# Router steps over more iterations, gate parts ahead of the subtractions, divisions ahead of weight pieces, other banks at the transition

## The chip, the cores and the metric

The kernel runs on one core of a Trainium2 chip. The metric is the device time of one execution in microseconds. The profile is one execution, taken by the hardware profiler. Its engines are TensorE (PE, and PEld for its weight loads), VectorE (DVE), ScalarE (ACT), GpSimd (POOL) and SyncE (SP, which issues most DMAs). Each engine works through its own queue in order.

## The reference

Attention over 8 batches of 576 tokens with 8 heads of 64: the first four heads see the last 32 positions, the last four see every 32nd position. The result, 4608 tokens of 512, goes through a mixture of experts: a token whose skip score is positive is given to the expert with the largest logit, passes its two layers, and the result times the gate is added to the token.

```python
scores = scale * q @ k.T, masked per head (local or strided)
attn = exp(scores - max);  attn = attn / (attn.sum(-1) + 1e-09)
x = (attn @ v) as [4608, 512]
do_compute = x @ w_skip > 0
e_idx = argmax(xc @ w_gate);  gate_w = softmax(xc @ w_gate)[e_idx]
h = relu(xc[mask] @ w1[e]);  y[mask] = gate_w * (h @ w2[e])      # 8 experts
out[do_compute] = xc + y
```

## The kernel before

**Attention.** The work of a batch is cut into four units `pr` 0 to 3 (`UNITS`): 0 and 1 are the local heads (5 and 4 blocks), 2 and 3 the strided heads (6 and 5 blocks). The loop at L860 runs over 32 iterations (b, pr). One iteration issues, in an order that each engine keeps:

- `qk` of the unit two iterations ahead: score matmuls into a pair of banks with the tag S (there is one such pair), the mask addition on VectorE that reads it (L211 local, L214 strided), the maximum (L220), and two subtractions on GpSimd (L222);
- `tex` of this unit: transposes (L242) and the exponential on ScalarE (L250);
- `score` of the batch before, in one iteration of each batch (L337, copies at L342 and L344);
- `xpose` of the unit two back: transposes of the finished x (L319) and copies (L321);
- `pv` of the unit one back: products with v (L276), then on VectorE the reciprocal of the sums (L285, L286) and the two divisions (L292), one for each bank of the pair PV.

**Router.** Every two batches make a group of nine tiles of 128 tokens. `route1` (end of batches 2, 4 and 6; for the last group at the transition) transposes the router scores (L361), finds each token's expert and leaves the sum of exponentials `zs`, made on GpSimd (L399 to L401). `route2` in (3,0), (5,0) and (7,0) (table `RANKS`) counts ranks with matmuls, takes the reciprocal of `zs` (L418), works out positions on VectorE (L420 to L432) and the gate in three bf16 parts on GpSimd (L435 to L440, `rpo` at L442). `onehots` (table `ONES`: (3,1), (5,1), (7,0)) makes two products on VectorE, `roh` (L453) and `rx` (L456); `rx` reads `rpo`. `tabled` (table `TABS`: (3,3), (5,3), (7,1)) multiplies them on TensorE (L464) and adds the result to `acc` (L468, L470). `pick` in (5,0) chooses an expert after batch 3 (L518 to L534); SyncE loads its number in (5,2) and uses it for the weight loads of this expert "e" (L602; three buffers `raw`). Its pieces are cast on ScalarE (`wcast`, L613) and the remainder made on VectorE (`wrest`, L619); `CASTS`, `RESTS` and `FETCH` say in which iterations. In (7,1) `chosen` takes the token indices of expert "e" from `acc` (`ei`, L492), and three indirect DMAs on GpSimd gather its tokens (L644).

**Transition (L920 to L934).** The last unit's products go to the pair S. Its divisions come after the remainder of weight piece 4; then piece 5 is cast and its remainder made, the gathered tokens are turned (`xturn`, L666 to L669) around the turn of the last x, and the last scores are made (L337).

**FFN.** A second PSUM pool (L937) has four banks S, three T and one R; its places follow the order in which the tags are first asked for. The first FFN matmuls of expert "e" (`ffn1a`, L711, L715; outputs at L684, L685) come first, then `route1`'s second half for the last group, `route2`, `onehots`, `tabled`. From about 187 us on the kernel runs through the experts' two layers (L672 to L674) to its end.

## Time and profile before

| what | us |
|---|---|
| median of 3 runs (lowest, highest) | 438.48 (437.18, 439.31) |
| the profiled execution | 436.99 |
| its span, first to last instruction | 435.2 |
| TensorE busy in it | 401.0 |
| VectorE busy in it | 272.2 |
| ScalarE busy in it | 202.5 |
| GpSimd busy in it | 125.6 |

The profiled execution is 1.8 us longer than its span; sums over the trace are made against it, and the median lies 1.5 us above it. Attention takes the first 160 us, the transition and the last group's router the next 27, the experts the rest.

### The profile page before, as it was taken

To read this page: it belongs to the slowest core of one execution; us is meant where nothing else is said; L and a number is where in the kernel's file an instruction comes from. 1 tells how busy PE (TensorE), PEld (TensorE's weight loads), DVE (VectorE), ACT (ScalarE), POOL (GpSimd) and SP (SyncE) were. 2 spreads that over 40 slices of the span, in tenths; PEclk is the share of its full clock that TensorE was granted. 3 is DMA by queue.
4 is the path that set the end of the run, shared out by engine and by line. 5 is a ranking of instruction groups with operands and counts; after the bars stand their busy time and mean duration, and the time that the engine had idled before them with its cause. 6 is when DMAs were issued, how large, how long until landed. Compare 5 with 4: busy or idle time off the path is not lost.

```text
span 435.2 us, 12084 instructions
## 1 busy us (share of the span) xinstructions
PE 401.0 (92%) x4975; PEld 364.2 (84%) x4976; DVE 272.2 (63%) x548; ACT 202.5 (47%) x384; POOL 125.6 (29%) x161
## 2 busy tenths in 40 slices
PE   5989799897879687999999999999999999999994
PEld 3878777787667464899898899999999999999984
DVE  3676669878968854872694563474564754755610
ACT  1557546584577255404533353544444445545300
POOL 2442334435323540250133144032042141201201
PEclk9799989999999878999999999999999999999999
DMA  8999978998896246034376567366466566636101
GB/s 278 397 386 313 316 233 274 304 291 296 258 372 196 58 137 172 2 104 131 104 234 187 164 222 193 132 202 205 149 201 191 161 215 194 205 130 196 42 20 44
DMA packets 49707, 86.05 MB, mean 198 GB/s; under 512 B 7050, under 2 KB 26890, under 8 KB 49648
## 3 DMA queue, kind: packets, MB, share of 16 engines
q1 hardware_dynamic: 43248, 74.87, 53.3%
q0 software_dynamic: 6400, 10.36, 8.3%
q8 instruction: 40, 0.66, 0.6%
q14 instruction: 19, 0.16, 0.1%
HBM read 70.88 MB, written 14.90 MB: 197 GB/s over the span
## 4 chain that ended last, share of the span: by engine, by line
PE 76%; DVE 14%; issue 3%; DMA 2%; ACT 2%; POOL 1%; SPq 1%; POOLq 0%; DVEq 0%
PE S L672 16%; PE S L674 16%; PE S L673 16%; PE PV L276 5%; PE T L242 5%; PE S L204 5%; PE T L319 3%; DVE x L292 2%; PE T L666 2%; PE PV L764 2%; PE T L337 2%; DMA kt<-in_kp_dram 1%; DVE mx L220 1%; DVE rx L456 1%; DVE frame L214 1%
## 5 line engine op out<-in xcount | busy, mean ns | idle before, releaser
L672 PE MATMUL S<-xh,w1h 128*128 128x342 f32 (+6 forms) x248 | 78.1, 315 | 0.0
L674 PE MATMUL S<-xh,w1l 128*128 128x342 f32 (+6 forms) x248 | 76.4, 308 | 0.0
L673 PE MATMUL S<-xl,w1h 128*128 128x342 f32 (+6 forms) x248 | 76.4, 308 | 0.0
L672 PE MATMUL S<-hh,w2h 128*128 128x288 f32 (+5 forms) x192 | 59.3, 309 | 0.6 <-DVE hl L685 0.6
L674 PE MATMUL S<-hh,w2l 128*128 128x288 f32 (+5 forms) x192 | 58.0, 302 | 0.0
L673 PE MATMUL S<-hl,w2h 128*128 128x288 f32 (+5 forms) x192 | 57.8, 301 | 0.0
L684 ACT ACTIVATE hh<-S 128x342 fp32r<-128x342 f32 (+6 forms) x64 | 27.8, 436 | 63.5 <-PE S L674 58.4
L752 POOL DMA_INDIRECT out_dram<-ot,n1i x18 | 19.3, 1070 | 116.9 <-DVE ot L750 115.4
L619 DVE TENSOR_TENSOR w1l<-raw,w1h 128x1024 fp32r<-128x1024 f32 x32 | 39.0, 1223 | 18.5 <-ACT w1h L613 17.7
L672 PEld LDWEIGHTS S<-xh,w1h 128*128 128x128 f32 x248 | 46.8, 189 | 0.3 <-issue 0.2
L673 PEld LDWEIGHTS S<-xl,w1h 128*128 128x128 f32 x248 | 46.7, 188 | 0.1
L674 PEld LDWEIGHTS S<-xh,w1l 128*128 128x128 f32 x248 | 46.7, 188 | 0.0
L619 DVE TENSOR_TENSOR w2l<-raw,w2h 128x1024 fp32r<-128x1024 f32 x32 | 39.1, 1223 | 10.0 <-ACT w2h L613 8.9
L204 PE MATMUL S<-kt,qt 64*64 64x54 f32 (+1 forms) x1280 | 34.7, 248 | 10.3 <-DMA kt<-in_kp_dram 3.5
L222 POOL TENSOR_TENSOR sm<-sm,mx 128x480 f32<-128x480 f32 (+1 forms) x32 | 28.4, 908 | 52.3 <-DVE mx L220 21.1
L204 PEld LDWEIGHTS S<-kt,qt 64*64 64x64 f32 x1280 | 29.0, 146 | 14.5 <-DVE sm L211 5.2
L685 DVE SCALAR_TENSOR_TENSOR hl<-S,hh 128x342 fp32r<-128x342 f32 (+6 forms) x64 | 30.5, 482 | 14.9 <-ACT hh L684 14.8
L250 ACT ACTIVATE ptl<-T 96x512 f32<-96x512 f32 (+1 forms) x40 | 19.9, 546 | 42.1 <-PE T L242 42.1
L672 PEld LDWEIGHTS S<-hh,w2h 128*128 128x128 f32 x192 | 36.2, 188 | 0.8 <-DVE hl L685 0.8
L673 PEld LDWEIGHTS S<-hl,w2h 128*128 128x128 f32 x192 | 36.3, 189 | 0.0
L674 PEld LDWEIGHTS S<-hh,w2l 128*128 128x128 f32 x192 | 36.1, 188 | 0.0
L730 ACT COPY yT<-S 128x288 f32<-128x288 f32 (+5 forms) x24 | 9.9, 412 | 55.9 <-PE S L674 47.0
(215 smaller groups left out, 813.3 us busy)
## 6 DMA issues: line engine op xcount, KB each, us to landing
raw<-in_w_dram SPq DMA_DIRECT2D x64, 512.0 KB
vt<-in_vp_dram SPq DMA_DIRECT2D x24, 390.0 KB
qt<-in_qp_dram SPq DMA_DIRECT2D x16, 304.0 KB
kt<-in_kp_dram SPq DMA_DIRECT2D x16, 297.0 KB
out_dram<-x SPq DMA_DIRECT2D x16, 288.0 KB
kt<-in_kp_dram SPq DMA_DIRECT2D x14, 304.0 KB
qt<-in_qp_dram SPq DMA_DIRECT2D x14, 288.0 KB
out_dram<-x SPq DMA_DIRECT2D x32, 99.0 KB
```

Of the source, the lines that this page charges most:

```text
L204: T.matmul(s[HP * (i ^ j):HP * (i ^ j) + HP, j, (blk - b0) * win:(blk - b0 + 1) * win], lhsT=qt[p, j, blk * nq:blk * nq + HP], rhs=kt[p, j ...
L222: G.tensor_tensor(e[:, j], e[:, j], mx[:, j].unsqueeze(2).broadcast_to([128, b1 - b0, win]), op=ALU.subtract)
L242: T.transpose(t[:w, x * 128:(x + 1) * 128], a, ident)
L250: A.activation(pt[:w, (g + x) * 128:(g + y) * 128], t[:w, x * 128:y * 128], AF.Exp, scale=0.125)
L276: T.matmul(p[HP * i:HP * i + HP, bank, slot * 65:slot * 65 + 65], lhsT=pt[a:z, m, j, i ^ j, :], rhs=vt[a:z, b0 // 2 + m if kind else (b0 + ...
L619: V.tensor_tensor(lo, raw_.pop((key, j)), hi.bitcast(F32), op=ALU.subtract)
L672: T.matmul(p, lhsT=a[0], rhs=b[0], start=start, stop=False)
L673: T.matmul(p, lhsT=a[0], rhs=b[1], start=False, stop=False)
L674: T.matmul(p, lhsT=a[1], rhs=b[0], start=False, stop=stop)
L684: A.activation(s["hh"][:, f, :C], p[:, :C], AF.Relu)
L685: V.scalar_tensor_tensor(s["hl"][:, f, :C], p[:, :C], 0.0, s["hh"][:, f, :C].bitcast(F32), op0=ALU.max, op1=ALU.subtract)
L752: i = G.indirect_dma_start(out=out, in_=ot[:P], in_offset=None, bounds_check=NTOK - 1, oob_is_err=False, out_offset=bass.IndirectOffsetOnA ...
```

## The change

- `scaled` makes one division in place of two where both banks hold the same number of slots: units 0, 1 and 2 of every batch; unit 3 keeps two.
- `gated` is cut out of `route2`: the reciprocal, the gate's parts and `rpo`. In (3,0), (5,0) and (7,0) it is issued within `qk`, after the mask addition and ahead of the maximum and the subtractions; for the last group ahead of the FFN's first outputs.
- `operands` (`rx`) is cut out of `onehots` and gets a table of its own; `onehots` and `tabled` move to later iterations, `pick` from (5,0) to (5,1), `chosen` and the gathers from (7,1) to (7,2).
- At the transition the last divisions come directly after their products, ahead of the remainder of piece 4; the cast of piece 4 moves there from (7,3); the cast and remainder of piece 5 move behind all turns of the gathered tokens.
- A tile of tag T and one of tag R are asked for ahead of the FFN's sums, so that T and R take the first four banks of the pool and S the last four.

```diff
--- before.py
+++ after.py
@@ -43,13 +43,14 @@
 ESTR = 5120
 ROUND = 1.5 * 2.0 ** 23
 RANKS = {(3, 0): 0, (5, 0): 1, (7, 0): 2}
-ONES = {(3, 1): 0, (5, 1): 1, (7, 0): 2}
-TABS = {(3, 3): 0, (5, 3): 1, (7, 1): 2}
+ONES = {(3, 1): 0, (5, 2): 1, (7, 1): 2}
+OPERANDS = {(3, 2): 0, (5, 3): 1, (7, 1): 2}
+TABS = {(4, 0): 0, (6, 0): 1, (7, 2): 2}
 COUNTED = {1: 3, 2: 5}
 PB = 3
 CB = 5
 EG = 2
-CASTS = [(6, 0), (6, 1), (7, 0), (7, 2), (7, 3)]
+CASTS = [(6, 0), (6, 1), (7, 0), (7, 2)]
 RESTS = [(6, 1), (6, 2), (7, 2), (7, 3)]
 FETCH = [(6, 0), (6, 1), (6, 3), (7, 0), (7, 3)]
 CE = (96, 3)
@@ -264,13 +265,11 @@
         if kind == 0:
             jobs = [(0, LW, m, j, j, m) for m in range(n) for j in range(2)]
             slots = (n, n)
-            outs = [x[:, :, 64 * j:64 * j + 64] for j in range(2)]
         else:
 
             jobs = [(HP * o, HP * o + SQ, m, j, o, 2 * m + j) for m in range((n + 1) // 2)
                     for o in range(2) for j in range(2) if 2 * m + o < n]
             slots = (n + 1) // 2 * 2, n // 2 * 2
-            outs = [x[:, o::2, :].rearrange("p m (j d) -> p m j d", j=2) for o in range(2)]
         for a, z, m, j, bank, slot in jobs:
             for i in range(2):
                 T.matmul(p[HP * i:HP * i + HP, bank, slot * 65:slot * 65 + 65], lhsT=pt[a:z, m, j, i ^ j, :],
@@ -284,12 +283,20 @@
             u = slots[z.start]
             V.tensor_scalar_add(rc[:, z, 0:u], pw[:, z, 0:u, 64], 1e-9)
             V.reciprocal(rc[:, z, 0:u], rc[:, z, 0:u])
-        for o in range(2):
-            u = slots[o]
-            num, den = pw[:, o, 0:u, 0:64], rc[:, o, 0:u].unsqueeze(2).broadcast_to([128, u, 64])
+        def scaled(to, z, u):
+            num = pw[:, z, 0:u, 0:64]
+            den = rc[:, z, 0:u].unsqueeze(3).broadcast_to([128, z.stop - z.start, u, 64])
             if kind:
-                num, den = (y.rearrange("p (m j) d -> p m j d", j=2) for y in (num, den))
-            V.tensor_tensor(outs[o], num, den, op=ALU.mult)
+                num, den = (y.rearrange("p o (m j) d -> p o m j d", j=2) for y in (num, den))
+            V.tensor_tensor(to, num, den, op=ALU.mult)
+
+        if kind == 0:
+            scaled(x.rearrange("p n (j d) -> p j n d", j=2), slice(0, 2), n)
+        elif n % 2 == 0:
+            scaled(x.rearrange("p (m o) (j d) -> p o m j d", o=2, j=2), slice(0, 2), w)
+        else:
+            for o in range(2):
+                scaled(x[:, o::2, :].rearrange("p m (j d) -> p m j d", j=2).unsqueeze(1), slice(o, o + 1), slots[o])
 
     def store(b, kind):
         ob = out[b * S:(b + 1) * S, kind * 256:kind * 256 + 256]
@@ -401,8 +408,25 @@
         G.tensor_scalar(zs, zs, 1e-9, None, op0=ALU.add)
         rt_[g] = [nt, sp, ohb, h, zs, tally if last else None]
 
+    def gated(g):
+        nt, sp, ohb, h, zs, tally = rt_[g]
+        at = slice(GA[g], GA[g] + nt)
+        gate = gates[:, at]
+        V.reciprocal(gate, zs)
+        p3 = pc[:, at]
+        G.tensor_copy(p3[:, :, 2], gate)
+        r = sp("rr", [128, nt])
+        G.tensor_tensor(r, gate, p3[:, :, 2], op=ALU.subtract)
+        G.tensor_copy(p3[:, :, 3], r)
+        G.tensor_tensor(r, r, p3[:, :, 3], op=ALU.subtract)
+        G.tensor_copy(p3[:, :, 4], r)
+        po = sp("rpo", [128, nt, 5, NE], BF16)
+        G.tensor_tensor(po, p3.unsqueeze(3).broadcast_to([128, nt, 5, NE]),
+                        ohb.unsqueeze(2).broadcast_to([128, nt, 5, NE]), op=ALU.mult)
+        rt_[g][4] = po
+
     def route2(g, tag="T", of=None):
-        nt, sp, ohb, h, zs, tally = rt_[g]
+        nt, sp, ohb, h, po, tally = rt_[g]
         rk = ps(tag)
         rkv = rk[:, 0:nt * NE].rearrange("p (t e) -> p t e", e=NE)
         T.matmul(rkv, lhsT=tri, rhs=ohb, start=True, stop=False)
@@ -414,8 +438,6 @@
             summed(of, rk[:, nt * NE:(nt + 1) * NE])
         yield
         at = slice(GA[g], GA[g] + nt)
-        gate = gates[:, at]
-        V.reciprocal(gate, zs)
         dd = sp("rdd", [128, nt, NE])
         V.tensor_tensor(dd, rkv, ohb, op=ALU.mult)
         ds = dsall[:, at]
@@ -431,16 +453,6 @@
         V.scalar_tensor_tensor(m3, nv, -3.0, ds, op0=ALU.mult, op1=ALU.add)
         V.tensor_tensor(n3, m3.unsqueeze(2).broadcast_to([128, nt, 3]),
                         con["n3"].unsqueeze(1).broadcast_to([128, nt, 3]), op=ALU.is_equal)
-        p3 = pc[:, at]
-        G.tensor_copy(p3[:, :, 2], gate)
-        r = sp("rr", [128, nt])
-        G.tensor_tensor(r, gate, p3[:, :, 2], op=ALU.subtract)
-        G.tensor_copy(p3[:, :, 3], r)
-        G.tensor_tensor(r, r, p3[:, :, 3], op=ALU.subtract)
-        G.tensor_copy(p3[:, :, 4], r)
-        po = sp("rpo", [128, nt, 5, NE], BF16)
-        G.tensor_tensor(po, p3.unsqueeze(3).broadcast_to([128, nt, 5, NE]),
-                        ohb.unsqueeze(2).broadcast_to([128, nt, 5, NE]), op=ALU.mult)
         rt_[g] = nt, sp, nv, n3, po
         if of is not None:
             counted(of)
@@ -452,6 +464,10 @@
         oh = sp("roh", [128, nt, 128], BF16)
         V.tensor_tensor(oh, con["iota"].unsqueeze(1).broadcast_to([128, nt, 128]),
                         nv.unsqueeze(2).broadcast_to([128, nt, 128]), op=ALU.is_equal)
+        rt_[g] = nt, sp, oh, n3, po
+
+    def operands(g):
+        nt, sp, oh, n3, po = rt_[g]
         x = sp("rx", [128, nt, 5 * NE, 3], BF16)
         V.tensor_tensor(x, po.rearrange("p t k e -> p t (k e)").unsqueeze(3).broadcast_to([128, nt, 5 * NE, 3]),
                         n3.unsqueeze(2).broadcast_to([128, nt, 5 * NE, 3]), op=ALU.mult)
@@ -875,7 +891,12 @@
         g = [i for i, x in enumerate(GROUPS) if x[1] == b]
 
         if n + LA < len(units):
-            run(qk(*units[n + LA]))
+            x = qk(*units[n + LA])
+            next(x)
+            next(x)
+            if (b, pr) in RANKS:
+                gated(RANKS[b, pr])
+            run(x)
         run(tex(b, pr))
         if b > 0 and pr == 2 + (b == NB - 1):
             run(score(b - 1))
@@ -896,9 +917,11 @@
         run(*front, *steps, *late)
         if (b, pr) in ONES:
             onehots(ONES[b, pr])
+        if (b, pr) in OPERANDS:
+            operands(OPERANDS[b, pr])
         if pr == 0:
             vodd(b)
-        if b == PB + 2 and pr == 0:
+        if b == PB + 2 and pr == 1:
             pick(PB)
         if (b, pr) in RESTS:
             j = RESTS.index((b, pr))
@@ -914,20 +937,19 @@
         if (b, pr) in FETCH:
             j = FETCH.index((b, pr)) + 1
             wdma("e", e0, j, j + 1)
-        if b == CB + 2 and pr == 1:
+        if b == CB + 2 and pr == 2:
             chosen(merged(acc[0], "e"), first.unsqueeze(1), [("e", *CE)], "e")
             gather("e", "e", "e", last=(CB + 1) * S)
     pool_order.close()
     nr = len(GROUPS) - 1
     with tc.manual_schedule(engines={T.engine, A.engine, V.engine, G.engine}):
         last, turn = pv(*units[-1], tag="S"), route1(nr)
-        next(last)
-        wrest("e", 4, 5)
-        run(xpose(*units[-2]))
+        run(last, xpose(*units[-2]))
         next(turn)
-        run(last)
+        wsplit("e", 4, 5)
+        run(xturn("e", 0, 2), xpose(*units[-1]), xturn("e", 2, 4))
         wsplit("e", 5, 6)
-        run(xturn("e", 0, 2), xpose(*units[-1]), xturn("e", 2, 4), score(NB - 1))
+        run(score(NB - 1))
     store(NB - 1, 0)
     wdma("e", e0, 6, 7, st_["e"]["taken"])
     store(NB - 1, 1)
@@ -935,15 +957,19 @@
     pctx.close()
     pctx = ExitStack()
     psum, bufs = pctx.enter_context(tc.tile_pool(name="psumT", bufs=1, space=PSUM, reuse_waits="tile")), {"S": 4, "T": 3, "R": 1}
+    ps("T"), ps("R")
     ga = ffn1a("e")
     with tc.manual_schedule(engines={T.engine, A.engine, V.engine, G.engine}):
-        run(islice(ga, 8), turn, ga)
+        run(islice(ga, 8), turn)
+        gated(nr)
+        run(ga)
         actx.close()
         pool["b"] = ctx.enter_context(tc.tile_pool(name="bpool", bufs=1, reuse_waits="tile"))
         wcast("e", 6, 7)
         g = ffn1("e", 2, 6)
         run(islice(g, 4), later(route2, nr))
         onehots(nr)
+        operands(nr)
         wcast("e", 7, 8)
         run(islice(g, 8))
         wrest("e", 6, 7)
```

## Rows read from the trace of the kernel before

**Rows 1.** The page, part 1: busy us and share of the span.
```profile
...
PE 401.0 (92%) x4975; PEld 364.2 (84%) x4976; DVE 272.2 (63%) x548; ACT 202.5 (47%) x384; POOL 125.6 (29%) x161
...
```

**Rows 2.** Stretches (4,1); (7,0)-(7,1); (7,2): us, busy PE PEld DVE ACT POOL, PEclk, DMA, GB/s.
```profile
...
86.30:89.90 3.60, 3.56 (x95) 3.15 (x87) 2.69 (x8) 2.14 (x5) 1.40 (x3) 1.00 0.99 343
...
142.50:150.30 7.80, 4.66 (x103) 3.95 (x104) 6.55 (x20) 1.75 (x4) 4.44 (x8) 0.98 0.28 78
150.30:155.80 5.50, 4.59 (x45) 3.78 (x43) 3.55 (x15) 0.87 (x2) 2.45 (x3) 0.50 0.01 1
...
```

**Rows 3.** Timeline, batch 3: start, us, engine, line; in brackets the idle time before.
```profile
...
75.89 1.27 DVE L456 TENSOR_TENSOR rx<-rpo,rn 128x1080 bf16<-128x1080 bf16 x1
...
77.08 1.15 DVE L211 TENSOR_TENSOR sm<-S,cs 128x960 f32<-128x960 f32 x1
...
78.28 0.89 PE L204 MATMUL S<-kt,qt 64*64 64x96 f32 x32 [0.77 <-DVE sm L211]
...
```

**Rows 4.** Timeline, batch 5: pick's first and last of seven, SyncE's weight load, two waits.
```profile
...
106.50 0.17 DVE L518 SCALAR_TENSOR_TENSOR key<-cnt,cs 128x8 f32<-128x8 f32 x1
...
107.90 0.14 DVE L534 CAST isel<-fsel 1x1 int32<-1x1 f32 x1
...
108.72 1.16 PE L204 MATMUL S<-kt,qt 64*64 64x96 f32 x40 [0.44 <-DVE frame L214]
109.07 0.35 SPq L602 DMA_DIRECT2D raw<-in_w_dram  x1
...
114.33 0.89 PE L204 MATMUL S<-kt,qt 64*64 64x96 f32 x32 [0.76 <-DVE sm L211]
...
```

**Rows 5.** Timeline, batch 7 up to the first turn of the gathered tokens.
```profile
...
146.00 1.42 POOL L440 CAST pc<-rr 128x9 bf16<-128x9 f32 x1
146.00 1.35 DVE L453 TENSOR_TENSOR roh<-cs,rnv 128x1152 bf16<-128x1152 f32 x1
147.50 0.79 POOL L442 TENSOR_TENSOR rpo<-pc,ohall 128x360 bf16<-128x360 bf16 x1
...
149.66 0.81 PE L464 MATMUL T<-rx,roh 128*128 128x120 bf16 x9 [2.98 <-DVE rx L456]
...
152.66 1.30 PE L319 MATMUL T<-cs,x 128*128 128x128 f32 x5 [0.91 <-DVE x L292]
...
153.92 0.17 DVE L492 CAST ei<-ey 128x6 int32<-128x6 f32 x1
154.39 1.21 POOL L644 DMA_INDIRECT xg<-out_dram,ei  x1 [1.74 <-DVE ei L492]
...
155.91 0.98 POOL L644 DMA_INDIRECT xg<-out_dram,ei  x1 [0.31 <-issue]
...
157.20 1.91 POOL L644 DMA_INDIRECT xg<-out_dram,ei  x1 [0.30 <-issue]
...
163.06 1.14 PE L666 MATMUL T<-cs,xg 96*128 96x96 f32 x6
...
```

**Rows 6.** Timeline, the transition.
```profile
...
165.66 0.90 PE L319 MATMUL T<-cs,x 128*128 128x128 f32 x5 [1.46 <-ACT xh L668]
...
172.58 0.40 PE L711 MATMUL S<-xh,w1h 128*128 128x288 f32 x1 [0.89 <-ACT s L344]
...
173.83 0.50 PE L361 MATMUL T<-cs,s 41*128 41x41 f32 x5
...
```

**Rows 7.** Timeline of TensorE, start of the FFN's second half.
```profile
...
190.87 0.40 PE L672 MATMUL S<-hh,w2h 128*128 128x288 f32 x1 [0.57 <-DVE hl L685]
...
```

**Rows 8.** Groups by line and shape: count, busy us, mean ns of one.
```profile
...
L292 DVE TENSOR_TENSOR x<-PV,rc 128x384 f32<-128x384 f32 x23 | 11.9, 545 | 0.5
...
L211 DVE TENSOR_TENSOR sm<-S,cs 128x768 f32<-128x768 f32 x8 | 7.6, 950 | 0.0
...
```

**Rows 9.** DMA queues, 158.5 to 159 and 162.5 to 163: the gathers' queue, packets, MB, share.
```profile
...
q0 software_dynamic: 4, 0.00, 0.5%
...
q0 software_dynamic: 7, 0.01, 6.4%
...
```

## The prediction

> **What bounds the kernel now.** I read the page first: TensorE is busy for 401 of 435.2 us, VectorE for 272 [rows 1]. From about 187 us on TensorE is full, and nothing of the change touches that part, so what is won or lost before it is carried to the end. Then the stretches by iteration: in an iteration without router work, (4,1), TensorE is busy 3.56 of 3.60 us and VectorE 2.69, so VectorE has 0.9 us to spare; in (7,0) to (7,1) TensorE is busy 4.66 of 7.80, and the stretch after it runs at half clock (0.50, that is 1.2 GHz) [rows 2]. Then the timeline of the router iterations for what TensorE waited on. In batch 3 VectorE runs the one-hot `roh`, the operands `rx` (1.27) and the mask addition of (4,0) in a row, and the scores of (4,1), which need the bank that this addition reads, start 0.77 late [rows 3]. In batch 5 seven instructions of `pick` (106.50 to 108.04) stand ahead of the addition of (5,3); the scores wait 0.44 for that one and 0.76 for the next [rows 4]. In batch 7 it is worst: route2, roh and rx of group 2 stand in one iteration, the cast at L440 lies beside `roh` and takes 1.42, rx waits for it, and the table's matmuls wait 2.98 for rx; the half clock follows, and 0.91 more for a division [rows 5]. At the transition TensorE stands 1.46 before the turn of (7,3)'s x and 0.89 in the middle of the first FFN matmuls [rows 6], and 0.57 for `hl` at 190.87 [rows 7].
>
> All moments below are on the clock of this trace; shifts from earlier parts come off in the sum.
>
> **Batch 3: rx and the table one iteration later.** No instruction is added. Without rx ahead of it the addition of (4,0) ends at 78.23 - 1.19 = 77.04 (rx starts at 75.89, the addition at 77.08), before TensorE is there: the 0.77 goes [rows 3]. rx then stands between the division of (3,1) and the addition of (4,1). VectorE's sum up to there is the same, so that addition comes no sooner than now and holds the scores of (4,2) a little, and the table's nine matmuls, some 0.6, move behind them. Bounds: 0.2 (nearly all given back) and 1.2 (a whole rx). I take 0.6, near the wait that is seen.
>
> **Batch 5: pick, roh, rx and table spread over four iterations.** Ahead of the addition of (5,3) 1.5 us of pick go, ahead of (6,0) roh and rx (2.6), while pick comes there (1.5). Both waits, 0.44 and 0.76, go [rows 4]; following VectorE's order with the durations of rows 3 to 5, the scores of (6,1) start 1.4 sooner, and by (6,3), behind rx and the table, 1.3 are left. Bounds: 0.6 (half of the two waits) and 2.0. I take 1.3. What pick delays is `isel`: SyncE can load its value only at about 111.1, so the first weight load (109.07 now) and the loads behind it on that queue go some 3 us later [rows 4]. Their covers are the iterations up to (7,0), whose q and k are read at 127: I cost it at nothing; uncovered it would be up to 3.0.
>
> **Gate parts ahead of the subtractions.** Six POOL instructions (five small ones and rpo with 0.79 [rows 5]) now hold the next subtraction on POOL by 1.1 to 1.5. Its reader, the transposes of tex, comes two iterations later. In batches 3 and 5 there is over 2 us of room; in (7,2) the subtraction would end at 146.4, TensorE comes at 146.7: nothing, but only just; without that room up to 1.4, and then it falls into the wait for the gather below. The reciprocal moves ahead of the reduction, 0.12 that VectorE pays anyway.
>
> **One division in place of two.** A 768-element addition out of PSUM takes 0.95, two divisions of 384 take 0.545 each and overlap a little (1.02 together) [rows 8]. So a merged one saves some 0.07; 24 of them save 1.7 us of VectorE time, of which only those in router iterations count. I put that into the terms above, not by itself.
>
> **Batch 7.** TensorE is done with (7,0)'s products at 149.66 - 2.98 = 146.68 [rows 5]. VectorE, which starts roh at 146.00, will instead do the restart (0.3), the addition and maximum of (7,3) (1.4) and the division of (7,0) (1.2): done at 149.0 instead of 152.5, so the turn of x starts 3.6 sooner than 152.66. Then roh and rx to 151.5, the table, the division of (7,1) to 152.5, the sum of the table 0.3, the weight remainder 1.2, and the eight small steps of `chosen` (some 1.4): the indices are ready at about 155.0, against 154.09 now (`ei`) [rows 5], 0.9 later. So TensorE's work would reach the first turn of the gathered tokens, 163.06 now, at 158.7, but the tokens are not there: this is what is late next. The three gathers hold POOL for 4.72 (154.39 to 159.11) [rows 5], so the third leaves POOL at about 160.0. Its landing is the unknown cost. The second left POOL at 156.89 and its last packets moved between 158.5 and 159: 2.0. The third left at 159.11 and moved its last between 162.5 and 163: 3.9, beside other queues [rows 9]. I take 2.0, because the weight piece and the store that went beside it wait for a remainder that now ends 3 to 4 us sooner. Start at 162.0 instead of 163.06: 1.1 gained; with 3.9 it would be 163.9, 0.8 lost.
>
> The Trainium skill (DMA: Bandwidth & Descriptors, section "Anatomy of one DMA — SWDGE (gpsimd) path") gives a DMA of this path about 2.0 us plus its bytes over 436 GB/s. For 96 rows of 2 KB that is an estimate of 2.45, and the sum below would be 5.4 instead of 5.8. The second gather's 2.0 is near it, the third's 3.9 is not.
>
> **Transition.** From that turn to route1's second transposes it is now 163.06 to 173.83, 10.8 us [rows 6]. The division of (7,3) no longer stands behind two weight remainders: x is there before TensorE, and 1.46 goes. With T and R placed first, the FFN's sums lie on banks that the last score does not use: the 0.89 before the second half goes. Against that, the cast of piece 5 (1.05) now stands on ScalarE ahead of the score's copies and holds them by up to 0.6. And TensorE will come out of 3.3 us of waiting; the 2.98 in batch 7 were followed by half clock [rows 2, 5]. Waits alone: 1.46 + 0.89 = 2.35; the cast takes up to 0.6 of it, and the earlier x lets ScalarE and VectorE do the copies between without a break, which gives about as much back. I take 2.3; bounds 1.3 (half clock throughout) and 3.6 (full clock throughout, which this stretch now has only in part).
>
> **Banks of the FFN's second half.** The 0.57 at 190.87 [rows 7] is a bank whose reader `hl` is late; the same product now lies on a bank of T, read long before: 0.5, bounds 0 and 0.6.
>
> **Sum.** 0.6 + 1.3 + 1.1 + 2.3 + 0.5 = 5.8 us. The profiled execution takes 436.99 us (435.2 of span and 1.8 around it), so 431.2 there. It lies 1.5 below the median of the runs, 438.48, against which I forecast: 432.7.
>
> **Rivals.**
> - *The gather lands late.* If it takes 3.9 again, the start is 0.8 late, the half clock follows (1.6 at the transition): 0.6 + 1.3 - 0.8 + 1.6 + 0.5 = 3.2, so 435.3. For it: the one row at this place. Against it: the neighbours on the DMA engines have moved away.
> - *The spread gives nothing back before batch 7.* VectorE has no less work, only in another order; if every moved step meets the next wait, the first two terms are 0: 3.9, so 434.6. For it: VectorE has under 1 us to spare in each iteration [rows 2]. Against it: the waits named are gone, and it can't gather more than the room.
> - *Both, or a change that does not act* (sums that stay on the old banks, waits that reappear under another name): 0 to 2 us, 436.5 to 438.5.
> - *Slower: the merged division is dear.* Its operands are walked in one more level, and rows of before have no such instruction. If it cost 0.9 more than the pair it replaces, plain iterations would hide it (0.9 of room [rows 2]), but batches 3, 5 and 7 have three each in iterations where VectorE is full: 9 x 0.9 = 8.1, against 5.8: 2.3 slower, 440.8. It decides from 0.65 per division on. Against it: the cost of VectorE's rows goes with the element count, whatever the shape [rows 8].
>
> **Chances.** Forecast 0.60, gather late 0.15, spread gives nothing 0.10, both or no effect 0.09, slower 0.06. A measurement tells about 0.5% (2.2 us) from no change: faster is 0.60 + 0.13 + 0.09 = 0.82, same 0.12, slower 0.06. Lower end: all upper bounds of the last three terms and a gather that lands at once, about 9 us, 429.5. Upper end: takes in the late gather and the spread without gain together with part of the third case, 436.8.
>
> **What would show it.** In the changed profile: no wait of about 0.8 before the scores of (4,1) and (6,1); no 2.98 before the table of group 2; its rx without a wait for POOL; TensorE waiting for a DMA, not for VectorE, before the first turn of the gathered tokens, for 2 to 5 us; no wait for the score's copies within the first FFN matmuls; merged divisions at 0.68 to 0.95. I would be wrong if merged divisions take over 1.5, if POOL's subtraction holds tex of (7,2), if late q and k hold the scores in batch 7, or if after the gather TensorE runs at half clock for much longer than 6 us.

## The result, and the profile after

The changed kernel takes 431.74 us, median of four runs (430.49 to 433.73), beside 438.18 for the kernel before (one run more than in the first table): a ratio of 0.985, 95% interval 0.981 to 0.990. A second, longer measurement on another occasion (the last experiment below) gives 434.73 beside 437.11, a ratio of 0.995, 0.991 to 0.998. Medians are over all runs of a kernel; ratios leave out runs more than 1.5% above its fastest. The forecast was 432.7. Both lie within its range, but the two intervals do not meet: the change is worth 0.5 to 1.5%, and the terms of the forecast's sum did not all come out.

The page of the changed kernel, part 1: TensorE's busy time falls by 1.7 us, VectorE's rises by 1.1 with 24 instructions fewer [rows 1].

```profile
...
PE 399.3 (93%) x4975; PEld 361.3 (84%) x4976; DVE 273.3 (64%) x524; ACT 203.4 (47%) x384; POOL 125.7 (29%) x161
...
```

I followed one set of marks through all profiles: the start of the score matmuls of each unit (b, pr) (L204 before and in e8, L205 in the others), and the first matmul of the FFN's second half. A time between two marks leaves out what an execution lost ahead of the first. All kernels of this study, in us; the last column is the time at half clock (granted clock 0.50, 1.2 GHz) within the stretch of the column before it:

```
kernel                (3,2)-(4,2) (3,2)-(4,3) (4,3)-(5,2) (5,2)-(7,0) (7,3)-FFN 2nd  half clock
before                   18.99       22.36       12.02       28.90       44.44         10.2
changed                  18.36       23.01       14.45       27.01       41.49         10.2
changed again            18.43       23.08       11.93       27.05       44.99         17.1
e1  gate behind          17.63       22.28       14.43       27.29       41.41          6.8
e2  old banks            18.43       23.08       11.77       27.03       42.04         10.2
e3  old transition       18.38       23.04       13.02       27.05       42.72         10.2
e4  no spread            19.61       22.98       11.89       30.32       41.96         10.2
e5  two divisions        18.44       22.99       14.35       27.13       45.16         17.1
e6  gather early         18.42       23.07       11.77       27.04       44.06         17.1
e7  gate and gather      17.64       22.29       15.71       26.36       43.11         10.2
e8  transition only      18.99       22.36       11.90       29.19       41.25         10.2
e9  spread in batch 5    18.92       22.28       11.96       29.35       41.37         10.2
e10 tokens last          17.63       22.28       14.40       26.35       45.51         10.2
```

The profiled executions differ by 5.0 us (436.99 and 431.98). By marks: 3.0 before the scores of (3,2), where nothing is changed; then 0.65 lost, 2.43 lost, 1.89 gained, 0.29 lost (up to (7,3)), 2.95 gained, and 0.52 gained behind. Now the rows.

Batch 3, timeline of the changed kernel (answers [rows 3]):

```profile
...
67.76 1.42 POOL L223 TENSOR_TENSOR frame<-frame,mx 128x324 f32<-128x324 f32 x2
68.02 0.50 DVE L450 TENSOR_SCALAR rnv<-dsall 128x9 f32<-128x9 f32 x1
...
68.55 0.65 DVE L451 TENSOR_SCALAR rnv<-rnv 128x9 f32<-128x9 f32 x1
...
75.09 0.89 PE L205 MATMUL S<-kt,qt 64*64 64x96 f32 x32
...
76.81 1.32 DVE L472 TENSOR_TENSOR rx<-rpo,rn 128x1080 bf16<-128x1080 bf16 x1
...
78.06 0.95 DVE L212 TENSOR_TENSOR sm<-S,cs 128x768 f32<-128x768 f32 x1
...
79.06 1.02 PE L205 MATMUL S<-kt,qt 64*64 64x54 f32 x48 [0.48 <-DVE sm L212]
...
83.13 0.65 PE L480 MATMUL T<-rx,roh 128*128 128x120 bf16 x9
...
```

The 0.77 before the scores of (4,1) is gone, and rx stands one addition later, as worked out; 0.48 comes back at (4,2), and the table at 83.13 now lies between the scores of (4,2) and (4,3). What was not foreseen is in the first three rows. GpSimd's subtraction begins at 67.76, later than before because of the gate's parts, and now runs beside two tiny instructions of route2 on VectorE. They take 0.50 and 0.65 for nine elements; in a kernel without this overlap both take 0.17 (e1 below). The same pair stands at 105.47 and 143.55.

A stop of TensorE behind it, in the same timeline:

```profile
...
83.14 1.42 POOL L223 TENSOR_TENSOR frame<-frame,mx 128x324 f32<-128x324 f32 x2 [1.39 <-DVE mx L221]
...
84.44 0.31 PE L243 MATMUL T<-cs,sm 128*96 128x128 f32 x1
...
...
87.23 0.97 PE L243 MATMUL T<-cs,sm 128*96 128x128 f32 x7 [2.48 <-POOL frame L223]
...
```

Eight transposes of tex (4,1) break off after the first one for 2.48 us. The named releaser, GpSimd's subtraction of another unit, started at 83.14 and was over at 84.56, and the transposes do not read its tile. In the DMA queues of the stretch 84.71 to 84.96 (packets, MB, share) stands one packet of an instruction queue:

```profile
...
q8 instruction: 1, 0.02, 22.5%
...
```

It comes 1.0 after the scores of (4,3) began, as the stop begins (84.75). What that says is seen against the same program without the stop (e11 below).

Batch 5 (answers [rows 4]): the scores of (6,1) at 112.61 wait for nothing, those of (6,0) wait 0.78 and those of (6,2) 0.55. SyncE issues the first weight load at 111.97, 2.9 later than before, and no wait for q, k or weights follows.

```profile
...
107.83 1.15 PE L205 MATMUL S<-kt,qt 64*64 64x96 f32 x40 [0.78 <-DVE frame L215]
...
111.97 0.35 SPq L618 DMA_DIRECT2D raw<-in_w_dram  x1
...
112.61 0.89 PE L205 MATMUL S<-kt,qt 64*64 64x96 f32 x32
...
116.47 0.75 PE L205 MATMUL S<-kt,qt 64*64 64x54 f32 x33 [0.55 <-DVE sm L212]
```

Batch 7 (answers [rows 5]): the table waits 0.69 in place of 2.98, x of (7,0) is turned at 148.23 in place of 152.66. Against the scores of (7,3) the gathers start 2.0 later than before (13.84 behind them, 11.87 before), where the forecast had 0.9; the third leaves GpSimd at 158.60, and its tokens hold TensorE until 162.09.

```profile
...
148.23 0.74 PE L326 MATMUL T<-cs,x 128*128 128x128 f32 x5 [1.93 <-DVE x L291]
...
149.41 1.27 DVE L472 TENSOR_TENSOR rx<-rpo,rn 128x1080 bf16<-128x1080 bf16 x1
...
150.74 1.08 PE L480 MATMUL T<-rx,roh 128*128 128x120 bf16 x9 [0.69 <-DVE rx L472]
...
154.35 0.17 DVE L508 CAST ei<-ey 128x6 int32<-128x6 f32 x1
...
154.83 1.21 POOL L660 DMA_INDIRECT xg<-out_dram,ei  x1 [6.55 <-DVE ei L508]
...
157.64 0.96 POOL L660 DMA_INDIRECT xg<-out_dram,ei  x1 [0.30 <-issue]
...
162.09 0.55 PE L682 MATMUL T<-cs,xg 96*128 96x96 f32 x4 [1.06 <-DMA xg<-out_dram,ei]
...
```

The transition (answers [rows 6]): x of (7,3) is there before TensorE, and the first FFN matmuls run without a wait in the middle.

```profile
...
162.48 0.71 PE L326 MATMUL T<-cs,x 128*128 128x128 f32 x5
...
166.70 0.61 PE L727 MATMUL S<-xh,w1h 128*128 128x288 f32 x1
...
169.32 0.50 PE L368 MATMUL T<-cs,s 41*128 41x41 f32 x5
...
```

Stretches of the changed kernel (answers [rows 2]; the last three columns are granted clock, DMA share, GB/s). After waits of 1.93 and 0.69, TensorE runs at half clock from 151 to 157, at full clock to 163.6, and, after waits of 1.06, 1.06 and 0.50, at half clock again.

```profile
...
150.99:156.99 6.00, 5.68 (x51) 3.35 (x50) 3.26 (x12) 2.18 (x6) 1.86 (x2) 0.50 0.40 116
157.20:163.60 6.40, 3.87 (x97) 3.12 (x91) 5.20 (x12) 5.90 (x13) 1.10 (x2) 1.00 0.54 159
163.60:167.40 3.80, 3.71 (x25) 2.00 (x26) 2.64 (x5) 2.48 (x7) 0.00 (x0) 0.55 0.70 212
...
```

The merged divisions, by shape (x count, busy us, mean ns): 0.96 and 0.69, and 0.82 for 640 elements.

```profile
...
L291 DVE TENSOR_TENSOR x<-PV,rc 128x768 f32<-128x768 f32 x8 | 7.7, 958 | 0.5
...
L291 DVE TENSOR_TENSOR x<-PV,rc 128x512 f32<-128x512 f32 x8 | 5.5, 692 | 0.3
...
```

### The profile page after: what moved, and what is told of

It reads as the page before. It is cut to its first block, busy times and chain, and to the rows that moved or that the text cites. A ratio compares the mean times of both kernels' runs of the same rounds, so it can differ in the third digit from the quotient of the medians.

```text
span 430.2 us, 12064 instructions
## 1 busy us (share of the span) xinstructions
PE 399.3 (93%) x4975; PEld 361.3 (84%) x4976; DVE 273.3 (64%) x524; ACT 203.4 (47%) x384; POOL 125.7 (29%) x161
## 4 chain that ended last, share of the span: by engine, by line
PE 72%; DVE 13%; DMA 6%; issue 4%; ACT 2%; SPq 1%; POOL 1%; POOLq 0%; DVEq 0%; ACTq 0%
PE S L688 17%; PE S L690 17%; PE S L689 17%; PE PV L275 4%; PE T L243 4%; PE S L205 3%; DVE x L291 2%; PE T L326 2%; PE T L682 2%; PE PV L780 2%; DMA vt<-in_vp_dram 2%; DVE mx L221 2%; DMA out_dram<-x 1%; DMA kt<-in_kp_dram 1%; PE T L344 1%
## 5 line engine op out<-in xcount | busy, mean ns | idle before, releaser
L635 DVE TENSOR_TENSOR w2l<-raw,w2h 128x1024 fp32r<-128x1024 f32 x32 | 39.1, 1223 | 10.5 <-ACT w2h L629 10.4
L223 POOL TENSOR_TENSOR sm<-sm,mx 128x480 f32<-128x480 f32 (+1 forms) x32 | 30.5, 976 | 51.4 <-PE T L326 19.1
L205 PE MATMUL S<-kt,qt 64*64 64x54 f32 (+1 forms) x1280 | 32.8, 240 | 8.1 <-DVE sm L212 3.5
L701 DVE SCALAR_TENSOR_TENSOR hl<-S,hh 128x342 fp32r<-128x342 f32 (+6 forms) x64 | 30.5, 481 | 14.9 <-ACT hh L700 14.8
L205 PEld LDWEIGHTS S<-kt,qt 64*64 64x64 f32 x1280 | 27.3, 139 | 12.4 <-DVE sm L212 4.2
```

The source lines that it names most:

```text
L205: T.matmul(s[HP * (i ^ j):HP * (i ^ j) + HP, j, (blk - b0) * win:(blk - b0 + 1) * win], lhsT=qt[p, j, blk * nq:blk * nq + HP], rhs=kt[p, j ...
L223: G.tensor_tensor(e[:, j], e[:, j], mx[:, j].unsqueeze(2).broadcast_to([128, b1 - b0, win]), op=ALU.subtract)
L635: V.tensor_tensor(lo, raw_.pop((key, j)), hi.bitcast(F32), op=ALU.subtract)
L701: V.scalar_tensor_tensor(s["hl"][:, f, :C], p[:, :C], 0.0, s["hh"][:, f, :C].bitcast(F32), op0=ALU.max, op1=ALU.subtract)
```

## The experiments

**e1: the gate's parts behind the subtractions.**

```diff
-            if (b, pr) in RANKS:
-                gated(RANKS[b, pr])
 (in route2, after its matmuls)
+        gated(g)
```

> The changed kernel with one part undone: the reciprocal, the gate's six POOL instructions and rpo stand in route2 again, behind the two subtractions on POOL. Theory: ahead of the subtractions they push these beside route2's two tensor_scalar instructions on VectorE (0.50 and 0.65 us in (3,0), (5,0), (7,0) of the changed kernel, 0.17 to 0.22 before), about 0.8 us of VectorE in each of three batches; undone, these two take 0.17 to 0.25 again, and the kernel is 0.5 to 2 us faster than the changed one (430 to 431 against before's 438.2). Rival: the move ahead is needed, because rx then waits for rpo as it did before; then the table of group 2 waits for POOL by 1 us or more and the kernel is 1 to 3 us slower than the changed one.

Measured: 432.37 median, ratio to before 0.985 (0.979 to 0.991). Timeline, the rows that answer to the first three of batch 3:

```profile
...
69.10 1.42 POOL L223 TENSOR_TENSOR frame<-frame,mx 128x324 f32<-128x324 f32 x2 [1.21 <-PE S L205]
...
70.41 0.17 DVE L452 TENSOR_SCALAR rnv<-dsall 128x9 f32<-128x9 f32 x1
...
70.62 0.17 DVE L453 TENSOR_SCALAR rnv<-rnv 128x9 f32<-128x9 f32 x1
...
```

Both instructions take 0.17 again. From the scores of (3,2) to (4,3) it takes 22.28 in place of 23.01, the same in e7 and e10, which have this edit too. In batch 5, e7 and e10 show 26.36 and 26.35 in place of 27.01 to 27.05; e1 has a stop of 1.13 there. So the place ahead of the subtractions costs 0.7 in each of these batches, and rx does not wait for rpo without it. In batch 7 it holds the gathers, which start 12.93 after the scores of (7,3) in e1 and 13.84 in the changed kernel; but e1's FFN starts its second half no sooner for it (41.41), though less of that stretch is at half clock. The total of e1 itself doesn't tell the two apart.

**e2: old banks.** The line `ps("T"), ps("R")` is left out.

> The changed kernel with one part undone: T and R are not asked for ahead of the FFN's sums, so these lie on the banks of the attention pool's S again. Theory: the wait in the middle of the first FFN matmuls for the score's copy comes back (0.89 in the kernel before) and 0.5 to 0.6 at the start of the FFN's second half; together 1.4 slower than the changed kernel. Rival: TensorE arrives from another place now, the copy is done 0.1 after the score and nothing is lost there: then only the 0.5 at the second half, or nothing, comes back.

Measured: 435.01, ratio 0.995 (0.992 to 0.999). The wait for the score's copy is back within the first FFN matmuls (0.69), the stretch to the FFN's second half is 0.55 longer than the changed kernel's at the same half clock, and the wait for `hl` is back behind it:

```profile
...
183.89 0.40 PE L688 MATMUL S<-hh,w2h 128*128 128x288 f32 x1 [0.55 <-DVE hl L701]
...
```

Together 1.1; the theory said 1.4.

**e3: old order at the transition.** The divisions of (7,3) stand behind the remainder of piece 4, and piece 5 ahead of the turns, as before the change.

> The changed kernel with one part undone: the last divisions stand behind the remainder of weight piece 4 again, and the cast and remainder of piece 5 ahead of the turns of the gathered tokens. Theory: TensorE waits some 1.5 us for x before the turn of (7,3)'s x, the kernel is 1 to 1.5 us slower than the changed one. Rival: in the changed kernel the tokens land late and TensorE waits for the DMA at this place anyway; the old order then fits into that wait and costs under 0.5 us.

Measured: 431.11, ratio 0.988 (0.983 to 0.992). The stretch takes 42.72, 1.23 more than the changed kernel's; the total doesn't show it. TensorE waits 2.21 for the tokens at the first turn, so part of the old order does hide in that wait, as the rival said, but not most of it.

**e4: no spread.** The tables `ONES`, `OPERANDS`, `TABS`, `pick`, `chosen` and the gathers as in the kernel before; gate ahead, merged divisions and transition as changed.

> The changed kernel with one part undone: pick, the one-hots, rx, the tables, chosen and the gathers stand in the iterations of the kernel before. Theory (the spread is what gains in the batches): the waits of about 0.8 before the scores of (4,1), 0.4 and 0.8 in batch 5 come back, and some 2 us before the table of group 2: 0.6, 1.5 and 1 to 3 us, together 3 to 5 us slower than the changed kernel. Rival: with the gate ahead, rx finds rpo ready and the gathers go out earlier, so that batch 7 loses nothing or even gains, and the kernel is 1 to 2 us slower at most.

Measured: 432.76, ratio 0.992 (0.989 to 0.995). The old waits are back:

```profile
...
77.48 0.89 PE L205 MATMUL S<-kt,qt 64*64 64x96 f32 x32 [0.77 <-DVE sm L212]
...
114.32 0.89 PE L205 MATMUL S<-kt,qt 64*64 64x96 f32 x32 [0.76 <-DVE sm L212]
...
149.66 0.65 PE L480 MATMUL T<-rx,roh 128*128 128x120 bf16 x9 [2.62 <-DVE rx L472]
...
```

Yet from (3,2) to (4,3) it takes 22.98, the same as the changed kernel's 23.01 to 23.08. With e1 (spread, gate behind: 22.28), the kernel before (neither: 22.36) and e9 (no spread here, gate behind: 22.28), all four corners are known: in batch 3 the spread gives nothing, the gate ahead costs 0.7. In batch 5 the spread is worth 3.3, stops included (2.5 to 2.8 with the gate behind: before and e8 against e7 and e10), and in batch 7, with the new transition, 0.5. By the marks that is 3.8, within the theory's 3 to 5; the total lies between the two measurements of the changed kernel and doesn't show it.

**e5: two divisions.** `scaled` is called for each bank of all units.

> The changed kernel with one part undone: two divisions for each unit again. Theory (the merged one saves 0.06 to 0.07 a unit, and only router iterations feel it): the pairs take 1.02, 0.89 and 0.76 again in place of 0.96, 0.82 and 0.69; from the scores of (3,2) to those of (4,2) 0.1 to 0.3 us longer than the changed kernel's 18.36; in all 0.2 to 0.8 us slower. Rival: TensorE waits elsewhere and nothing changes, within 0.1 us over that stretch.

Measured: 433.66, ratio 0.993 (0.990 to 0.996). From (3,2) to (4,2) it takes 18.44, against 18.36 to 18.43 with the merged one: 0.0 to 0.1. The rival is nearer.

**e6: gathers ahead of weight piece 2.**

```diff
+        if b == CB + 2 and pr == 2:
+            chosen(...); gather(...)
         if (b, pr) in RESTS:
             ...
-        if b == CB + 2 and pr == 2:
-            chosen(...); gather(...)
```

> The changed kernel, with chosen and the gathers ahead of the remainder of weight piece 2 in (7,2). Theory: the first gather starts 1.2 us sooner against the scores of (7,3) (12.6 after them, the changed kernel 13.84), its tokens land 6.9 to 7.3 us after that, the wait of 1.06 for the DMA goes, and the FFN's second half starts 0.5 to 1.2 us sooner against the scores of (7,3) than the changed kernel's 41.49. Rival: the turns then wait for the remainder or for x instead, and it starts within 0.3 us of that.

Measured: 434.19, ratio 0.995 (0.992 to 0.999). The first gather starts 12.85 after the scores of (7,3), and TensorE waits for no DMA, but half clock lasts 17.1 in place of 10.2, and the stretch takes 44.06. Against the second profile of the changed kernel, with the same 17.1 of half clock, it is 0.9 sooner, as the theory said; but that is one execution against one.

**e7: e1 and e6 together.**

> The changed kernel with the gate's parts behind the subtractions again and the gathers ahead of the remainder of weight piece 2: what the other runs have shown to be better, together. Theory: from the scores of (3,2) to (4,2) 17.6 us as with the gate alone (changed kernel 18.36), from the scores of (7,3) to the FFN's second half 40.5 (41.4 with the gate alone); about 2 us faster than the changed kernel where neither has a stop of TensorE without a named cause. Rival: the gains fall into the wait for the tokens, and it equals the run with the gate alone.

Measured: 432.50, ratio 0.989 (0.986 to 0.993). The first stretch came out (17.64), the second did not (43.11). Timeline:

```profile
...
151.47 1.23 DVE L637 TENSOR_TENSOR w1l<-raw,w1h 128x1024 fp32r<-128x1024 f32 x1
151.87 1.91 POOL L662 DMA_INDIRECT xg<-out_dram,ei  x1 [5.33 <-DVE ei L510]
...
155.31 1.23 DVE L637 TENSOR_TENSOR w1l<-raw,w1h 128x1024 fp32r<-128x1024 f32 x1
155.37 2.00 POOL L662 DMA_INDIRECT xg<-out_dram,ei  x1 [0.30 <-issue]
...
158.90 0.39 PE L684 MATMUL T<-cs,xg 96*128 96x96 f32 x1 [2.16 <-DMA xg<-out_dram,ei]
...
160.75 1.38 PE L684 MATMUL T<-cs,xg 96*128 96x96 f32 x5 [1.46 <-DMA xg<-out_dram,ei]
...
```

The gathers start at 11.9 after the scores of (7,3), 1.0 sooner than in e1, but now a remainder of VectorE (L637) runs beside the first and the third, which take 1.91 and 2.00 in place of 1.21 and 0.96 in the changed kernel. The last tokens land 8.9 after the first gather, in place of 7.3. TensorE, which is ahead here, waits 2.16 and 1.46 for them.

**e8: the kernel before with the transition alone.** Its order and the banks are as in the changed kernel, all else as before.

> The kernel before with the transition alone changed: the order of the last divisions and of the pieces 4 and 5, and T and R ahead of the FFN's sums. Theory (as predicted: 2.3 and 0.5): 32.57 from the first gather to the FFN's second half become 30 to 30.5, and the 0.57 at its start goes, 2.5 to 3 us faster than before. Up to the scores of (7,3) it runs the instructions of the kernel before: by the theory that the stops without a named cause vary from execution to execution, single markers up to (7,0) lie up to 3 us apart from before's, but the stretch from the scores of (3,2) to (4,2) takes before's 18.99 within 0.2. Rival: these stops belong to the program, and all its markers up to (7,3) lie within 0.5 of before's.

Measured: 431.66, ratio 0.989 (0.986 to 0.993). TensorE's timeline, batch 7 and the transition:

```profile
...
146.51 1.08 PE L464 MATMUL T<-rx,roh 128*128 128x120 bf16 x9 [2.99 <-DVE rx L456]
...
160.68 0.71 PE L666 MATMUL T<-cs,xg 96*128 96x96 f32 x6
161.83 0.90 PE L319 MATMUL T<-cs,x 128*128 128x128 f32 x5 [0.44 <-DVE x L292]
...
180.62 0.30 PE L672 MATMUL S<-hh,w2h 128*128 128x288 f32 x1
...
```

With the whole 2.99 wait for rx, and the same 10.2 of half clock as before, the stretch from (7,3) to the FFN's second half is 41.25: 3.2 less than before, and not more than the changed kernel's 41.49. From the first gather (151.24) to the FFN's second half it takes 29.4, less than the 30 to 30.5 expected, and the median is 4.7 below before's, where 2.5 to 3 were expected. Up to (7,3) it runs the instructions of the kernel before. The stretches of batch 3 are equal to the hundredth (18.99, 22.36), but it reaches the scores of (3,2) 3.33 sooner: where the kernel before stopped for 1.59 and ran at a granted clock of 0.57 (54 to 58 us), e8 stopped for 0.50 and kept 1.00.

**e9: spread in batch 5 only, gate behind.**

```diff
-ONES = {(3, 1): 0, (5, 2): 1, (7, 1): 2}
-OPERANDS = {(3, 2): 0, (5, 3): 1, (7, 1): 2}
-TABS = {(4, 0): 0, (6, 0): 1, (7, 2): 2}
+ONES = {(3, 1): 0, (5, 2): 1, (7, 0): 2}
+OPERANDS = {(3, 1): 0, (5, 3): 1, (7, 0): 2}
+TABS = {(3, 3): 0, (6, 0): 1, (7, 1): 2}
```

The gathers stand in (7,1), the gate's parts in `route2`.

> The changed kernel with the gate's parts behind the subtractions, and the router steps of batches 3 and 7 in the iterations of the kernel before; only those of batch 5 and pick stay spread. Theory: the spread gained something only in batch 5, and in batch 7 the kernel before with the new transition was as quick as the changed one. From the scores of (3,2) to those of (4,3) 22.3 us (before 22.36, changed 23.01), from (5,2) to (6,3) 22.3 (before 25.17, changed 22.95), from (7,3) to the FFN's second half 41 to 41.5 (41.25 with the new transition alone). In all 1 to 2 us faster than the changed kernel. Rival: the stops without a named cause and the half clock decide, and the total can't be told from the changed kernel's.

Measured: 430.52, ratio 0.982 (0.977 to 0.986), its six runs from 426.21 to 431.14. Measured alongside it, the changed kernel, run again, has 0.995 (0.991 to 0.998): e9 beats both kernels there. The first measurement of the changed kernel, 0.985 (0.981 to 0.990), overlaps with e9's, and of the 4.2 between the two medians the marks put 0.8 down to batch 3 and, by e7 and e10, 0.7 to the gate in batch 5; what the rest belongs to is not shown. Batch 3 (22.28) and the transition (41.37) are as expected; in batch 5 the profiled execution, the longest of the six, had a stop of its own, and 3.4 us of half clock behind it, so the 22.3 did not come out there:

```profile
...
102.35 1.10 PE L205 MATMUL S<-kt,qt 64*64 64x54 f32 x27 [1.62 <-issue]
...
```

**e10: tokens last.** e1, and at the transition:

```diff
-        run(xturn("e", 0, 2), xpose(*units[-1]), xturn("e", 2, 4))
+        run(xpose(*units[-1]), score(NB - 1), xturn("e", 0, 4))
         wsplit("e", 5, 6)
-        run(score(NB - 1))
```

> The changed kernel with the gate's parts behind the subtractions, and at the transition the turn of (7,3)'s x and the last score ahead of all turns of the gathered tokens. Theory: the late tokens are what is left of the time at this place (waits of 1.06 in the changed kernel, 1.73 and 0.65 around the turns with the gate behind); some 2 us of TensorE's work now stand in this wait, and the FFN's second half starts 39 to 40.5 us after the scores of (7,3) (41.49 changed, 41.41 with the gate behind). Rival: TensorE then waits for the copies of the last x and its score instead, or runs longer at half clock, and the stretch takes 41 or more.

Measured: 435.21, ratio 0.994 (0.992 to 0.997). The stretch takes 45.51; the theory failed, as its rival said. Timeline:

```profile
...
162.74 2.46 PE L344 MATMUL T<-xT,w 128*32 128x288 f32 x16
...
166.03 1.28 ACT L351 COPY s<-T 32x288 f32<-32x288 f32 x2
...
167.37 0.47 PE L684 MATMUL T<-cs,xg 96*128 96x96 f32 x3 [1.28 <-ACT s L351]
...
179.79 0.17 PE L526 MATMUL R<-run,oneb 128*128 128x8 bf16 x1 [1.26 <-DVE run L393]
...
```

The last score runs mostly at half clock, as in the changed kernel; its copies now hold ScalarE ahead of the casts of the turned tokens, and the last turns wait 1.28 for a bank that the copies read. Later TensorE waits 1.26 for `run`, which `route1` makes on VectorE; e1 has no such wait. These two are 2.5 of the 4.1 that the stretch is longer than e1's; half clock is 3.4 longer too.

**e11: the changed kernel again.**

> The changed kernel once more, unaltered. Theory: the stretches set by waits come out as in its first profile within 0.15 us: 18.36 from the scores of (3,2) to (4,2), 18.31 from (5,2) to (6,2); the stops of TensorE without a named cause (2.48 at 84.75, 1.15 at 126) and the places of half clock before 64 us don't, so that its markers there lie up to 3 us away from those of the first profile. Rival: the program alone sets the stops, and they stand at the same places with the same lengths within 0.3 us.

Measured: 434.73, ratio 0.995 (0.991 to 0.998). The stretches set by waits are the same (18.43, and 18.33 from (5,2) to (6,2)). The stops of 2.48 and 1.15 are not there: (4,3) to (5,2) takes 11.93 in place of 14.45. The instruction queue's packet comes 1.9 before the scores of (4,3), not 1.0 after them (DMA queues, 82.54 to 82.79):

```profile
...
q8 instruction: 1, 0.02, 22.5%
...
```

It is so in all thirteen profiles: the packet comes 0.9 to 1.1 after the mark in the five with a stop of 2.15 to 2.48 there (changed, e1, e5, e7, e10), and each stop begins within 0.2 of it; it comes 1.4 to 2.0 before the mark in the eight without. So the stop goes with a packet of instructions that comes 2 to 3 us later; what makes it late is not shown. But half clock at the transition lasts longer: the granted clock is 0.87 over 145 to 185 in the first profile and 0.79 over 142 to 183 in this one (stretches, granted clock third from the right):

```profile
...
145.00:185.00 40.00, 33.53 (x355) 27.32 (x351) 30.77 (x92) 18.64 (x41) 7.69 (x16) 0.87 0.32 97
...
```

```profile
...
142.00:183.00 41.00, 34.72 (x338) 28.65 (x335) 28.49 (x77) 18.14 (x40) 7.29 (x15) 0.79 0.31 95
...
```

That is 0.13 x 40 x 2 = 10.4 us and 0.21 x 41 x 2 = 17.2 us at 1.2 GHz (10.2 and 17.1 in the table, which is not rounded on the way), and the stretch takes 44.99 in place of 41.49, more than before's 44.44. The program alone does not set either.

## Why the prediction was right, and where not

The time fell inside the range and near the forecast, but several terms missed and made up for each other.

- **Batch 3, 0.6: failed.** The gain was there at the scores of (4,2) (0.63, and 1.36 with the gate behind) and was gone at (4,3), where the table now stands. The step that failed is "I take 0.6, near the wait that is seen": the text itself said that VectorE's sum stays the same. The rival that the spread gives nothing back held here (0.1 with the gate behind). Stretches of before, changed and e9, from the scores of (3,2) to (4,3):

```profile
...
63.71:86.07 22.36, 19.96 (x520) 16.66 (x513) 20.56 (x51) 13.08 (x28) 10.75 (x21) 1.00 0.90 285
...
```

```profile
...
60.70:83.71 23.01, 20.93 (x524) 17.17 (x516) 21.37 (x49) 13.33 (x28) 12.04 (x21) 1.00 0.90 288
...
```

```profile
...
61.30:83.58 22.28, 20.41 (x519) 16.88 (x513) 20.41 (x47) 12.96 (x28) 10.78 (x21) 1.00 0.94 298
...
```

  VectorE is busy 20.56 of 22.36, 21.37 of 23.01, 20.41 of 22.28: the time follows its sum, with 1.6 to 1.9 left over in each, whatever the order; so it does in e1 (20.60 of 22.28) and e4 (21.14 of 22.98).
- **Gate ahead, cost nothing: failed.** I looked for who waits for the delayed subtraction, and rightly found nobody; I did not look at what the subtraction would now run beside. 0.7 in batch 3 and 0.7 in batch 5. The Trainium skill (SBUF — State Buffer, section "Who interferes with whom") says that VectorE's tensor_scalar can take the port pair that it shares with GpSimd, and that the loser is blocked for the other's whole instruction. The rows agree: of the two subtractions the first ends at 68.49 and the second at 69.18; the first tensor_scalar, started in the middle of the one, ends at 68.52, and the next, started within the other, at 69.20.
- **Batch 5, 1.3: right in kind, its size by luck.** 1.85 to 1.9 up to (7,0). Of this, 0.95 is a stop before the scores of (6,3), which stands there in all three profiles without the spread (0.95, 1.22, 1.45) and in none with it; the waits alone give 0.9, and 1.6 with the gate behind. At (6,3), for which the 1.3 was worked out, they give 1.27 without this stop, but 1.92 with the gate behind (e7, e10): the gate, costed at nothing, took the rest. Before has two more stops in this stretch (0.93 and 0.94, within the scores of (5,2) and (5,3)); e8, with one of 0.60 in their place, takes as long to (6,2), 20.69 against 20.67, so I count them at nothing.
- **Pick's loads, cost nothing: right.** They went 2.9 later, and nobody waited.
- **Merged divisions: right.** 0.06 to 0.07 a unit, nothing to be seen in the stretches.
- **Batch 7, 1.1, and transition, 2.3: right in sum, wrong in share.** 2.95 in the first profile against 3.4; but the transition and banks alone give 3.2 (e8), all without the transition's order 1.7 (e3), and everything no more than the transition. Taken singly, the order is worth 1.23 (e3), where 1.46 was counted, and the banks 0.55 (e2), where 0.89 was. The waits that I took out of batch 7 came back as a wait for the tokens, as the forecast said. The step that failed is "I take 2.0": TensorE went on 3.5 after the third gather left GpSimd, so nothing was left of the 1.1; its wait for the DMA is 1.06, where the forecast's sign was 2 to 5. That is nearer to the rival *the gather lands late* (3.9) than to the forecast. It is 1.0 above the estimate of 2.45 that the prediction worked out from the Trainium skill (DMA: Bandwidth & Descriptors, section "Anatomy of one DMA — SWDGE (gpsimd) path"). That the third gather left GpSimd only 1.0 later against the scores of (7,3) (17.61, before 16.59), near the forecast's 0.9, was luck: the first started 2.0 later, 0.9 of it through the gate's parts (e1), and the third took 0.96 where it took 1.91 before.
- **Banks, 0.5: right** (0.55 behind, and 0.55 within the first half, where 0.89 was counted).
- **Left out: what the executions add by themselves.** 3.0 of the 5.0 between the two profiles were lost by the kernel before ahead of the scores of (3,2), with 13.7 us at half clock there against 6.8; the changed kernel lost 2.48 in a stop behind batch 3. Such a stop, or 0.94 before (5,1), stands between (4,3) and (5,2) in six of the nine profiles with the table in (4,0), and in none of the four with the table in (3,3); whether the place of the table brings it is open, since nine and four are few. And a sign of being wrong that the forecast named, half clock after the gather "for much longer than 6 us", is there in the second profile of the changed kernel: 10.2 us from 158.6 on, and 3.4 in the first.

What the runs put down to the change is 0.65 lost in batch 3, 1.9 gained in batch 5, 2.95 at the transition at equal half clock, 0.5 behind: 4.7, less a stop of 2.2 to 2.5 in five of nine executions. The 0.5 is 0.05 in the second profile, where TensorE waits 0.52 for a later gather. The two measurements, 6.4 and 2.4 us, stand around that; it is a sum of stretches of single executions and not a measurement of its own.

## What to carry to other kernels

Before spreading work over iterations, add up each engine's time over the whole stretch up to where the next slack is: a wait that goes is a gain only if the engine that it waited for has room there (in batch 3 VectorE had 1.8 of 22.4 us left over before, and no order got below 1.5; in batch 5 it had 4.2 of 28.9, and 2.0 after). When an instruction is delayed on GpSimd, ask not only who waits for it, but also what VectorE runs beside it at its new place. And compare marks that lie behind every moved step, in more than one execution, before a change of 1% is put down to its parts.

## What the runs showed that was not expected

- A 128x9 tensor_scalar on VectorE takes 0.17 alone and 0.50 to 0.65 beside a GpSimd subtraction.
- The same program gave 10.2 and 17.1 us of half clock around the transition, and the stretch differs by 3.5 us. The Trainium skill (TensorE: Matmul & The Clock Gate, section "What's actually happening") says that the point at which the clock changes differs from run to run for one kernel; it speaks of a kernel's start. These two profiles show the same in the middle of one: half clock begins 9.3 us after the scores of (7,3) in the first, 6.8 in the second.
- TensorE stops for 0.4 to 2.5 us with no engine to blame, at places that partly belong to the program (1.45 at the same place within the scores of (7,0) in all three profiles without the spread; from none to 1.69 there in the nine with it) and partly to the execution (2.48 and none at 84 us in two profiles of one kernel, with the packet of instructions 3 us apart).
- An indirect gather's instruction on GpSimd takes 0.96 to 2.00 us, and what runs on VectorE goes with it: in all thirteen profiles the nine gathers that start beside the remainder of a weight piece take 1.69 to 2.00, the other thirty 0.96 to 1.22. From the start of a gather to its landing the profiles that show it have 3.2 to 6.1 us.
